# A recurrence followed by a token-and-channel mixer on one core: another order of the first batch's work, and another layout of the last branch

## The chip, the cores and the metric

The program runs on one core of a Trainium2 chip. The core has five engines with an instruction stream each: PE (TensorE, matrix products into PSUM banks), DVE (VectorE), ACT (ScalarE), POOL (GpSimd) and SP (SyncE, which here issues nearly all DMAs). [...] The metric is the device time of one launch in microseconds (us), the median of several runs; lower is better.

## The reference

```
for t in range(S):                                   # S = 768, batch 4, 8 heads of 48
    y[:, :, t] = r_t @ (state + (u * k_t) outer v_t)
    state = w_t[..., None] * state + k_t outer v_t
x = y, heads side by side                            # (4, 768, 384)
h = relu(x^T @ w_tok1) @ w_tok2                      # 768 -> 256 -> 768, over tokens
x = x + h^T
out = x + relu(x @ w_ch1) @ w_ch2                    # 384 -> 1536 -> 384, over channels
```

All is float32 for the kernel. The four weight matrices come as float64 and are turned to float32 on the chip.

## The kernel before

**Units.** The recurrence is cut into twelve units: a batch (4) times half of a sequence of 6 blocks of 128 tokens, so three units a batch (`UB = 3`, `NU = 12`; unit 0, 1, 2 are the first batch, written `e0`, `e1`, `e2`). A unit has four chunks of 64 tokens. `unit(i)` returns its steps as functions:

- `ends` (L351 to L357): a scan on DVE over the decays, and a reciprocal. `begins` (L364): a second scan. `keys` (L361) and `queries` (L367): products on DVE.
- `own_u` (L372, L264): four products by u on ACT. `own_gram`, `gram` (L248): 32 small products each on PE into a pair of banks of `ps_g`. `mask` (L406) and `own_put` (L260): DVE reads these into `at`.
- `tokens` (L278): eight turns of the keys on PE into two banks of `ps_m`; `copied` (L279): two copies to `kT` on ACT.
- `carry` (L295): the outer products `kv` of keys and values on PE. `scaled` (L419, four small ACT instructions) multiplies a state by the chunk's decay; `updates` (L429, DVE) adds the chunk's part of `kv` and makes the next state. So the chunks of a unit, and the units of a batch, form one chain: state, scaling, state.
- `before` (L308, PE: queries times states) and `after` (L322, PE: `at` times values) sum into one `y` in `ps_a`, a pool of one pair of banks, which most units' `kv` use too. Between the two stands the ACT copy `seen` (L314). `taken` (L328): three ACT copies of `y` into `x`.
- `ranges` (L348): two ACT instructions over 1041 columns, each of which sums up into `flags` whether a decay left the range in which this way of computing holds.

**Weights.** `convert` turns a block of float64 to float32: `load` (L197, two DMAs into `spare` or `scratch`), `exponent` (L200, DVE), `mantissa` (L206, DVE), `raise_two` (L203, ACT), `add` (L212, DVE), `signs` (L209, ACT) and `put` (L215 and two L218, DVE; L215 reads what L203 and L209 made). In the first batch's list these are `x`, `m`, `p`, `add`, `g`, `put` with the number of the block. Three blocks make the token weights, nine the channel weights (`to_ch`).

**Mixer.** `hidden` (L497, with L499 on ACT), `back` (L504 on PE, L506 on DVE adds to `x`), `turn` (L512, L513), `up` (L520 on PE, L522 on ACT) and `down` (L591), or `quarters` (L609), which makes a product with seven smaller ones, and the stores (L596, L613).

**Order.** `strict` gives PE, DVE and ACT exactly the order of the calls. For the three units of the first batch that order is one list written by hand (L700 to L709). SP's order is left to the scheduler of the language. After that list PSUM is dealt out anew (`ps_m` gets six banks), and for every batch `woven` merges lists of (cost, function) by the share of the cost sum that lies ahead of each: the next batch's unit steps among this batch's mixer pieces. `ahead` is the list of the first mixer's `turned` pieces, `both` that of its first 24 `up` pieces.

**End.** `verdict` sums `flags` on PE and DVE to one number. Every engine loads it (L768) and compares (L835). If a decay was out of range, everything is computed again in another way (`by_halves`, in a loop); with the inputs of the reference this doesn't happen. The layout is: compare, then an unconditional jump over the loop, which on each engine waits for that engine's own last work (on SP: for all DMA semaphores), then the loop's code, then the end (L868).

Of the kernel before, what the change touches and what calls it, by code (L numbers as in the profile page):

```python
# [10 lines left out]
f32 = mybir.dt.float32  # L11
bf16 = mybir.dt.bfloat16
i32 = mybir.dt.int32
# [15 lines left out]
ROWS = P + D  # L29
# [33 lines left out]
def rwkv6_then_mixer(  # L63
# [17 lines left out]
    nc = tc.nc  # L81
# [28 lines left out]
    def bank(name):  # L110
        return ps_m.tile([128, 512], f32, name=name, tag="m")
# [16 lines left out]
    def load_w(i):  # L128
        if i < NU:
            for cols in (slice(MID, WCOLS), slice(0, MID)) if i == 0 else (slice(0, WCOLS),):  # L130
                sp.dma_start(ws[i % 2][:, cols], w[i][:, cols])

    def load_rk(i):
        if i < NU:
            for n in (1, 0):
                for rows in (slice(0, 128),) if i < 3 else (slice(0, D), slice(P, P + D)):
                    sp.dma_start(rks[i % 3][rows, ts(n, COLS)], rk[i, n, rows, :])

    vs, nears = {}, {}

    def load_v(i):
        if i < NU:
            vs[i] = vpool.tile([128, UC, DM], f32, name="vt")
            b, j = divmod(i, UB)
            sp.dma_start(vs[i], v[b, ts(j, UC * 128), :].rearrange("(c p) e -> p c e", p=128))
# [138 lines left out]
            f()  # L284
        return kT

    def outer(kT, vt, half, where=None):

        where = where or (ps_a, "a")
        kv = where[0].tile([128, 2, 512], f32, name="kv_ps", tag=where[1])  # L290
        for c in range(UC):
            for a in range(A):
                for j, q in ((0, 0), (1, 1), (0, 1), (1, 0)):
                    if 2 * (half * UC + c) + j < 2 * C - 1:
                        pe.matmul(kv[ts(q, P), j, ds((c * A + a) * D, D)], kT[ts(j, T), c, a, ts(q, P)],  # L295
                                  vt[ts(j, T), c, ts(2 * a + q, D)], start=True, stop=True)
        return kv

# [31 lines left out]
    def unit(i):  # L330
# [75 lines left out]
                dve.tensor_mul(at[:, q], g, over_heads(strictly, g.shape[1]))  # L406

        def carry():
            L["kv"] = outer(L.pop("kT"), vs[i], half, (ps_g, "gram") if i == UB - 1 else (ps_a, "a"))

        def by_last(c, j):
            return of_chunks(L["to_end"], 1, 1)[:, :, 0].rearrange("p (x j) -> p x j", j=2)[:, ts(c, A), j]
# [8 lines left out]
        def update(c, j):  # L421
            g = 2 * (half * UC + c) + j
            if g < 2 * C - 1:
                new = state[bt, g + 1] = apool.tile([128, A, D], f32, name="state", bufs=3)
                got = L["kv"][:ROWS, j, ds(c * A * D, A * D)].rearrange("p (a e) -> p a e", a=A)
                if g == 0:
                    dve.tensor_copy(new[:ROWS], got)
                else:
                    dve.tensor_add(new[:ROWS], L["before"][g][:ROWS], got)  # L429
# [32 lines left out]
    def weight_sums(n):  # L462
        t1, t2, t4 = w_sums
        to, a, b = ((t1, w12, w11), (t2, w22, t1), (t4, w21, t2), (w12, w22, w12))[n]
        dve.tensor_sub(to, a, b)
# [203 lines left out]
    def steps(i):  # L669
# [29 lines left out]
    t0, t1, t2 = (e["scaled"] for e in (e0, e1, e2))  # L699
    strict(*e0["own_u"], e0["ends"], e0["own_gram"], e0["begins"], e0["keys"], e0["tokens"], *e0["copied"], e0["queries"], lambda: load_w(2),  # L700
           e0["gram"], *e1["own_u"], e1["ends"], e0["carry"], *e0["ranges"], e0["mask"], e0["own_put"], e1["own_gram"], s0[0], t0[1],
           x0, p0, s0[1], t0[2], m0, g0, e1["begins"], s0[2], t0[3], add0, s0[3], e0["before"], put0, load2,
           e1["keys"], e0["after"], *e0["taken"], e1["tokens"], *e1["copied"], e1["queries"], e1["gram"], *e2["own_u"], t1[0],
           e2["ends"], e1["carry"], lambda: load_v(2), e2["begins"], e1["mask"], e2["own_gram"], e1["own_put"], x1, p1, s1[0], t1[1],
           m1, g1, e2["keys"], s1[1], t1[2], e2["tokens"], e2["queries"], s1[2], t1[3], e2["gram"], *e2["copied"], h[0], h[1], add1, s1[3],
           t2[0], e1["before"], e2["mask"], e2["carry"], e1["after"], e2["own_put"], put1, s2[0], t2[1],
           *e1["taken"], h[2], h[3], x2, s2[1], t2[2], m2, p2, *h[4:6], add2, g2, s2[2], t2[3], *h[6:8], s2[3], e2["before"], put2, e2["after"],
           *e2["taken"], lambda: (load_w(3), load_rk(3), load_v(UB), load_w(4), load_rk(4)), to_ch[0][0], to_ch[1][0],
           *e1["ranges"], *h[8:], *e2["ranges"], lambda: sp.dma_start(u_rows, u_all))  # L709

    six_banks.close()
    ps_g, ps_m = None, six_banks.enter_context(tc.tile_pool(name="ps_m", bufs=6, space=bass.MemoryType.PSUM))
# [4 lines left out]
    flagged = []  # L717

    def verdict():
        total = bank("total")[0:1, :2 * NU]  # L720
        pe.matmul(total, ones, flags.rearrange("p i n -> p (i n)"), start=True, stop=True)
        of_all = const.tile([128, 1], f32, name="of_all")
        beyond = const.tile([128, 1], i32, name="beyond")
        dve.tensor_reduce(out=of_all[0:1], in_=total, axis=mybir.AxisListType.X, op=ALU.add)
        dve.tensor_scalar(beyond[0:1], of_all[0:1], 0.0, 1.0, op0=ALU.is_le, op1=ALU.is_lt)
        flagged.append(beyond)

    def last_mixing():
        hiddens, turned, rights, thirds, quarters = mixing_of(B - 1)
        of, sums = rights(0)  # L730
        *turned, end = turned
        pieces = [e for h in hiddens for e in h] + turned[:8] + sums[:4] + turned[8:10] + sums[4:8] + turned[10:] + sums[8:]
        ups = thirds(0, of)
        of, sums = rights(1)
        pieces += ups[:2] + [end] + ups[2:4] + woven(ups[4:], sums) + thirds(1, of)

        def third():
            L["of"], L["sums"] = rights(2)

        L = {}  # L740
        sums = [(0.05, lambda n=n: L["sums"][n][1]()) for n in range(12)]
        lefts_of = [(0.9, lambda n=n: L["ups"][n][1]()) for n in range(15)]
        pieces += [(0.01, third)] + woven(quarters(0), sums) + [(0.1, verdict), (0.01, lambda: L.update(ups=thirds(2, L["of"])))]
        return pieces + lefts_of + quarters(1) + quarters(2)

    for bt in range(B):
        ahead = []
        if bt == 0:
            to_ch = [single(e, n) for n, e in enumerate(to_ch)]
            both = [f for e in zip(ups[0], ups[1]) for f in e]  # L750
            ahead = woven(turned, sum(to_ch[:2], []))
            of_weights = [(0.1, lambda n=n: weight_sums(n)) for n in range(4)]
            pieces = woven(both, sum(to_ch[2:8], [])) + woven(downs[0][:6], to_ch[8]) + woven(downs[0][6:], of_weights[:3])
            pieces += downs[1][:4] + of_weights[3:] + downs[1][4:] + ups[2] + downs[2]
        elif bt < B - 1:
            hiddens, turned, ups, downs = mixing_of(bt)
            pieces = [e for h in hiddens for e in h] + turned
            *pieces, last = pieces
            ups[0].insert(2, last)
            for s in range(S // SEG):  # L760
                pieces += ups[s] + downs[s]
        else:
            pieces = last_mixing()
        n = (bt + 1) * UB
        att = [e for i in range(n, n + UB) if i < NU for e in steps(i)]
        strict(*(f for _, f in ahead + (woven(att, pieces) if att else pieces)))

    rare = nc.values_load(flagged[0][0:1, 0:1], min_val=0, max_val=1, skip_runtime_bounds_check_because="a comparison's result")  # L768

    def by_halves(b):  # L770

# [17 lines left out]
        for half in range(UB):  # L789
# [25 lines left out]
            for c in range(UC):  # L815
                for j in range(2):
                    g = 2 * (half * UC + c) + j
                    if g < 2 * C - 1:
                        new = states[g + 1] = apool.tile([128, A, D], f32, name="before", bufs=5)
                        got = kv[:ROWS, j, ds(c * A * D, A * D)].rearrange("p (a e) -> p a e", a=A)  # L820
                        if g == 0:
                            dve.tensor_copy(new[:ROWS], got)
                        else:
                            dve.tensor_mul(new[:ROWS], states[g][:ROWS], by[:, ts(c, A), j].unsqueeze(2).to_broadcast([ROWS, A, D]))
                            dve.tensor_add(new[:ROWS], new[:ROWS], got)
# [6 lines left out]
        for s in range(S // SEG):  # L832
            emit(ups[s] + downs[s])

    with tc.If(rare > 0, preferred_fallthrough_block=False):  # L835
        with tc.For_i(0, B, 1) as b:
            by_halves(b)

# [33 lines left out]
```

## Time and profile before

| what | value |
|---|---|
| median of 3 runs | 546.42 us (545.99 to 547.14) |
| the profiled execution | 544.09 us, of it 542.3 us span |
| busy in the span | PE 505.3, DVE 335.9, ACT 212.4, POOL 1.3 us |
| mean granted PE clock | 0.972 |
| DVE busy in 0:10, 10:20, 20:30, 30:40, 40:50, 50:60 | 6.93, 9.36, 9.90, 9.36, 9.09, 2.59 us |
| ACT busy in the same | 3.19, 7.93, 4.81, 6.67, 6.81, 8.20 us |
| PE busy in the same | 1.41, 6.93, 6.64, 6.11, 8.76, 7.59 us |
| granted PE clock in the same | 1.00, 0.85, 0.50, 0.67, 0.95, 1.00 |

The span reaches from the program's first instruction to its last; the launch around it makes the rest of the time. A share is an average over stages with different limits: the first 60 us hold the first batch's recurrence and the token weights, up to about 145 us the first mixer runs beside the channel weights' conversion and the second batch's units, and then three mixers follow, the first two of them with the next batch's units beside them. PE's busy time is modelled: 10.00 of 10 us doesn't mean that PE is at its peak.

### The profile page before, as it was taken

Reading aid. Unit: us, or ns where it says so; the run is one execution under the profiler, and the core shown is the slowest. Engines: PE = TensorE matmul, PEld = TensorE weight load, DVE = VectorE, ACT = ScalarE, POOL = GpSimd, SP = SyncE. Lnnn points to the kernel's source line nnn. Section 1 sums busy time; section 2 is a strip of 40 time slices with the busy share of each in tenths; the row PEclk is TensorE's granted clock in tenths of the full one; section 3 lists DMA queues with packets and bytes.
Section 4 is the critical chain, followed back from the end, with each engine's and each line's share of the span. In section 5 each row is a group of like instructions: output and inputs, shape, how many; then the busy total and the mean of one; then the engine's idle time right before and its main releaser. Section 6 shows DMA issues by size and latency. Waiting matters only on the chain.

```text
span 542.3 us, 12629 instructions
## 1 busy us (share of the span) xinstructions
PE 505.3 (93%) x5542; PEld 436.7 (81%) x5542; DVE 335.9 (62%) x514; ACT 212.4 (39%) x525; POOL 1.3 (0%) x10
## 2 busy tenths in 40 slices
PE   3578899899799999999899999999999999999995
PEld 3466478676798968898898967898898968999995
DVE  7998499878771754193381655286394625775653
ACT  3676876671233323424324333523414313531300
POOL 0000000000000000000000000000000000000000
PEclk9669999999999999999999999999999999999998
DMA  8968656623221404204123113002000000000000
GB/s 307 332 157 242 183 167 242 174 89 97 84 74 61 132 15 129 59 7 152 30 64 122 33 58 100 30 1 89 2 29 2 2 29 1 1 1 31 1 31 33
DMA packets 20941, 46.01 MB, mean 85 GB/s; under 512 B 2128, under 2 KB 13008, under 8 KB 20880
## 3 DMA queue, kind: packets, MB, share of 16 engines
q1 hardware_dynamic: 20736, 45.14, 26.1%
q8 instruction: 45, 0.74, 0.6%
q14 instruction: 16, 0.13, 0.1%
q10 hardware_dynamic: 144, 0.00, 0.0%
HBM read 40.41 MB, written 4.72 MB: 83 GB/s over the span
## 4 chain that ended last, share of the span: by engine, by line
PE 75%; DVE 15%; ACT 4%; DMA 3%; issue 2%; SPq 0%; DVEq 0%; ACTq 0%
PE q_ps L609 26%; PE z_ps L520 21%; PE z_ps L552 6%; PE h_ps L504 5%; PE h_ps L497 5%; PE y_ps L322 3%; PE y_ps L308 3%; DMA rk<-in_rk_dram 2%; PE gram L248 2%; DVE scratch L212 2%; PE kv_ps L295 1%; DVE wch L218 1%; PE k_ps L278 1%; DVE w L364 1%; PE xT_ps L512 1%
## 5 line engine op out<-in xcount | busy, mean ns | idle before, releaser
L520 PE MATMUL z_ps<-xT,wch 128*128 128x256 f32 x648 | 148.0, 384 | 0.0
L520 PEld LDWEIGHTS z_ps<-xT,wch 128*128 128x128 f32 x648 | 121.0, 190 | 16.6 <-DVE wch L218 0.3
L609 PE MATMUL q_ps<-wch,z 128*128 128x192 f32 x492 | 87.8, 330 | 0.0
L609 PEld LDWEIGHTS q_ps<-wch,z 128*128 128x128 f32 x492 | 81.1, 191 | 1.3 <-DVE z L651 0.3
L522 ACT ACTIVATE z<-z_ps 128x256 f32<-128x256 f32 x108 | 41.1, 381 | 84.0 <-PE z_ps L520 83.3
L419 ACT ACTIVATE before<-state,to_end 112x48 f32<-112x48 f32 x176 | 44.2, 324 | 32.6 <-DVE state L429 29.9
L609 PE MATMUL q_ps<-scratch,z 128*128 128x192 f32 x324 | 56.5, 327 | 0.2 <-DVE z L651 0.2
L609 PEld LDWEIGHTS q_ps<-scratch,z 128*128 128x128 f32 x324 | 53.0, 190 | 0.6 <-issue 0.4
L429 DVE TENSOR_TENSOR state<-before,kv_ps 112x192 f32<-112x192 f32 x40 | 14.0, 350 | 40.1 <-ACT before L419 28.1
L504 PE MATMUL h_ps<-h,wtok 128*128 128x384 f32 x96 | 35.4, 493 | 0.6 <-ACT h L499 0.6
L497 PE MATMUL h_ps<-x,wtok 128*128 128x384 f32 x96 | 32.5, 490 | 2.8 <-ACT x L328 2.6
L506 DVE TENSOR_TENSOR x<-x,h_ps 128x384 f32<-128x384 f32 x24 | 13.3, 553 | 34.1 <-PE h_ps L504 33.9
L619 DVE TENSOR_TENSOR o<-x,z 128x192 f32<-128x192 f32 x8 | 2.9, 359 | 49.2 <-ACT z L618 46.7
L497 PEld LDWEIGHTS h_ps<-x,wtok 128*128 128x128 f32 x96 | 17.8, 190 | 14.6 <-ACT x L328 3.4
L356 DVE TENSOR_TENSOR_SCAN to_end<-w,starts 112x1041 f32<-112x1041 f32 (+1 forms) x13 | 28.1, 2160 | 2.2 <-DMA w<-in_w_dram 1.8
L364 DVE TENSOR_TENSOR_SCAN w<-w,starts 112x1041 f32<-112x1041 f32 x12 | 27.9, 2321 | 0.1
L348 ACT ACTIVATE junk<-to_end,least 112x1041 uint8<-112x1041 f32 x12 | 14.0, 1163 | 28.3 <-DVE to_end L356 28.3
L504 PEld LDWEIGHTS h_ps<-h,wtok 128*128 128x128 f32 x96 | 16.6, 190 | 10.1 <-ACT h L499 2.8
L328 ACT COPY x<-y_ps 64x384 f32<-64x384 f32 (+1 forms) x36 | 17.1, 474 | 19.1 <-PE y_ps L322 18.8
L308 PEld LDWEIGHTS y_ps<-before,rk 48*64 48x64 f32 x704 | 13.5, 139 | 13.4 <-issue 8.0
L308 PE MATMUL y_ps<-before,rk 48*64 48x48 f32 x704 | 15.1, 227 | 9.6 <-DVE state L429 9.6
L513 ACT COPY xT<-xT_ps 128x384 f32<-128x384 f32 x24 | 11.4, 476 | 22.8 <-PE xT_ps L512 22.8
(136 smaller groups left out, 671.3 us busy)
## 6 DMA issues: line engine op xcount, KB each, us to landing
rk<-in_rk_dram SPq DMA_DIRECT2D x36, 192.0 KB, 4.1
near<-in_near_dram SPq DMA_DIRECT2D x8, 768.0 KB, 4.4
w<-in_w_dram SPq DMA_DIRECT2D x11, 520.5 KB, 3.4
spare<-in_w_ch_dram SPq DMA_DIRECT2D x10, 512.0 KB, 4.8
vt<-in_v_dram SPq DMA_DIRECT2D x12, 384.0 KB, 3.9
out_dram<-o SPq DMA_DIRECT2D x24, 192.0 KB, 1.9
scratch<-in_w_ch_dram SPq DMA_DIRECT2D x8, 512.0 KB, 4.6
rk<-in_rk_dram SPq DMA_DIRECT2D x6, 512.0 KB, 8.5
```

Of the source, the lines that this page charges most:

```text
L308: pe.matmul(y[put(q, j), q, ds((c * A + a) * D, D)], r_[q * P:q * P + D, ds((c * A + a) * 128 + j * T, T)], before[g][q * P:q * P + D, a, ...
L322: pe.matmul(y[put(q, j), q, ts(ca, D)], at[ts(j, T), q, ca, :], vt[ts(j, T), c, ts(2 * a + q, D)], start=False, stop=ca == 0, skip_group_c ...
L328: return [lambda: act.copy(x[:, 0], got[:, 0])] + [lambda n=n: act.copy(x[ts(n, P), 1], got[ts(1 - n, P), 1]) for n in range(2)]
L356: dve.tensor_tensor_scan(to, of, start, 0.0, op0=ALU.mult, op1=ALU.add)
L364: dve.tensor_tensor_scan(w_[:ROWS], w_[:ROWS], starts[:ROWS], 0.0, op0=ALU.mult, op1=ALU.add)
L419: act.mul(t[:ROWS, a], state[bt, g][:ROWS, a], by_last(c, j)[:, a:a + 1])
L497: pe.matmul(sums[i], wtok1[:, c, ts(i, 128)], x_of()[:, c, :], start=(c == 0), stop=(c == C - 1))
L504: pe.matmul(ps, wtok2[:, i, ts(c, 128)], h1[:, i, :], start=(i == 0), stop=(i == DTOK // 128 - 1))
L520: pe.matmul(ps, wch1[:, m, ts(jt, 128)], xT[:, m, ts(s, SEG)], start=(m == 0), stop=(m == DM // 128 - 1))
L522: act.activation(zs[s][:, jt, :], ps, AF.Relu)
L552: pe.matmul(ps[:, q], lefts[r][:, ts(q, 128)], of[r], start=first and q == 0, stop=end and q == JB - 1, skip_group_check=True)
L609: pe.matmul(ps, a[:, j, :], b[:, j, :], start=(j == 0), stop=(j == HJ - 1))
```

## The change

It has three parts.

1. **The first batch's list.** Unit 0's steps stay in place. Then the states of units 1 and 2 follow each other without conversions between unit 1's: `t1[0]` comes right after unit 0's last state, `e1["carry"]` goes ahead of unit 0's `taken`, unit 2's `own_u`, `ends`, `keys`, `tokens` and `carry` go ahead of unit 1's `before`; the second and third block of token weights move behind them. Unit 2's `kv` no longer takes a pair of banks of `ps_g` but two single banks of `ps_m`, so `outer` returns a list of two and its readers index it.
2. **Flag sums.** `ranges` of unit 1 leave the list for `ahead`, those of unit 2 for the first six pieces of `both`. The cost sums of both lists grow by that.
3. **The branch.** `verdict` yields 1 for within range, the compare jumps for that case to a block at the end of the code, and the loop is its other side. Four pieces ahead of the end of the last mixer's products PE gets a hint that names this jump as likely taken.

```diff
-    def outer(kT, vt, half, where=None):
-
-        where = where or (ps_a, "a")
-        kv = where[0].tile([128, 2, 512], f32, name="kv_ps", tag=where[1])
+    def outer(kT, vt, half, apart=False):
+
+        both = None if apart else ps_a.tile([128, 2, 512], f32, name="kv_ps", tag="a")
+        kv = [bank("kv_ps") if apart else both[:, j] for j in range(2)]
...
-           x0, p0, s0[1], t0[2], m0, g0, e1["begins"], s0[2], t0[3], add0, s0[3], e0["before"], put0, load2,
-           e1["keys"], e0["after"], *e0["taken"], e1["tokens"], *e1["copied"], e1["queries"], e1["gram"], *e2["own_u"], t1[0],
-           e2["ends"], e1["carry"], lambda: load_v(2), e2["begins"], e1["mask"], e2["own_gram"], e1["own_put"], x1, p1, s1[0], t1[1],
-           m1, g1, e2["keys"], s1[1], t1[2], e2["tokens"], e2["queries"], s1[2], t1[3], e2["gram"], *e2["copied"], h[0], h[1], add1, s1[3],
-           t2[0], e1["before"], e2["mask"], e2["carry"], e1["after"], e2["own_put"], put1, s2[0], t2[1],
-           *e1["taken"], h[2], h[3], x2, s2[1], t2[2], m2, p2, *h[4:6], add2, g2, s2[2], t2[3], *h[6:8], s2[3], e2["before"], put2, e2["after"],
-           *e2["taken"], lambda: (load_w(3), load_rk(3), load_v(UB), load_w(4), load_rk(4)), to_ch[0][0], to_ch[1][0],
-           *e1["ranges"], *h[8:], *e2["ranges"], lambda: sp.dma_start(u_rows, u_all))
+           x0, p0, s0[1], t0[2], m0, g0, e1["begins"], s0[2], t0[3], add0, s0[3], t1[0], e0["before"], put0, load2,
+           e1["keys"], e0["after"], *e2["own_u"], e1["tokens"], *e1["copied"], e1["queries"], e1["carry"], *e0["taken"], lambda: load_v(2),
+           e1["gram"], e2["ends"], e2["keys"], s1[0], t1[1], e2["tokens"], e2["begins"], e2["copied"][0], s1[1], t1[2], e2["copied"][1],
+           e2["carry"], e1["mask"], s1[2], t1[3], e1["own_put"], e2["own_gram"], s1[3], t2[0], e2["queries"], e2["gram"], e1["before"],
+           s2[0], t2[1], x1, p1, m1, e1["after"], s2[1], t2[2], e2["mask"], *h[:4], s2[2], t2[3], e2["own_put"], *e1["taken"], add1, g1,
+           s2[3], e2["before"], put1, to_ch[0][0], e2["after"], *h[4:8], x2, m2, *e2["taken"], p2, add2, g2, *h[8:], put2,
+           lambda: (load_w(3), load_rk(3), load_v(UB), load_w(4), load_rk(4)), to_ch[1][0], lambda: sp.dma_start(u_rows, u_all))
...
-        dve.tensor_scalar(beyond[0:1], of_all[0:1], 0.0, 1.0, op0=ALU.is_le, op1=ALU.is_lt)
+        dve.tensor_scalar(within_range[0:1], of_all[0:1], 0.0, None, op0=ALU.is_le)
...
+        ending = quarters(2)
+        ending.insert(-5, (0.01, lambda: tc.mark_branch_hint_location("by_halves", "LikelyTaken", [pe.engine])))
...
-            ahead = woven(turned, sum(to_ch[:2], []))
+            ahead = woven(turned, sum(to_ch[:2], []), [(1.3, f) for f in e1["ranges"]])
+            both = woven(both[:6], [(1.3, f) for f in e2["ranges"]]) + both[6:]
...
-    with tc.If(rare > 0, preferred_fallthrough_block=False):
+    with tc.If(common > 0, preferred_fallthrough_block=False, label="by_halves") as within_range:
+        pass
+    with within_range.Else():
         with tc.For_i(0, B, 1) as b:
             by_halves(b)
```

More of the change, by code (lines that the diff above doesn't have):

```diff
@@ L294, in outer @@
                     if 2 * (half * UC + c) + j < 2 * C - 1:
-                        pe.matmul(kv[ts(q, P), j, ds((c * A + a) * D, D)], kT[ts(j, T), c, a, ts(q, P)],
+                        pe.matmul(kv[j][ts(q, P), ds((c * A + a) * D, D)], kT[ts(j, T), c, a, ts(q, P)],
                                   vt[ts(j, T), c, ts(2 * a + q, D)], start=True, stop=True)
@@ L408, in carry @@
         def carry():
-            L["kv"] = outer(L.pop("kT"), vs[i], half, (ps_g, "gram") if i == UB - 1 else (ps_a, "a"))
+            L["kv"] = outer(L.pop("kT"), vs[i], half, apart=i == UB - 1)
         def by_last(c, j):
@@ L424, in update @@
                 new = state[bt, g + 1] = apool.tile([128, A, D], f32, name="state", bufs=3)
-                got = L["kv"][:ROWS, j, ds(c * A * D, A * D)].rearrange("p (a e) -> p a e", a=A)
+                got = L["kv"][j][:ROWS, ds(c * A * D, A * D)].rearrange("p (a e) -> p a e", a=A)
                 if g == 0:
@@ L722, in verdict @@
         of_all = const.tile([128, 1], f32, name="of_all")
-        beyond = const.tile([128, 1], i32, name="beyond")
+        within_range = const.tile([128, 1], i32, name="within_range")
         dve.tensor_reduce(out=of_all[0:1], in_=total, axis=mybir.AxisListType.X, op=ALU.add)
-        dve.tensor_scalar(beyond[0:1], of_all[0:1], 0.0, 1.0, op0=ALU.is_le, op1=ALU.is_lt)
-        flagged.append(beyond)
+        dve.tensor_scalar(within_range[0:1], of_all[0:1], 0.0, None, op0=ALU.is_le)
+        flagged.append(within_range)
     def last_mixing():
@@ L743, in last_mixing @@
         pieces += [(0.01, third)] + woven(quarters(0), sums) + [(0.1, verdict), (0.01, lambda: L.update(ups=thirds(2, L["of"])))]
-        return pieces + lefts_of + quarters(1) + quarters(2)
+        ending = quarters(2)
+        ending.insert(-5, (0.01, lambda: tc.mark_branch_hint_location("by_halves", "LikelyTaken", [pe.engine])))
+        return pieces + lefts_of + quarters(1) + ending
     for bt in range(B):
@@ L766, in rwkv6_then_mixer @@
         strict(*(f for _, f in ahead + (woven(att, pieces) if att else pieces)))
-    rare = nc.values_load(flagged[0][0:1, 0:1], min_val=0, max_val=1, skip_runtime_bounds_check_because="a comparison's result")
+    common = nc.values_load(flagged[0][0:1, 0:1], min_val=0, max_val=1, skip_runtime_bounds_check_because="a comparison's result")
     def by_halves(b):
@@ L819, in by_halves @@
                         new = states[g + 1] = apool.tile([128, A, D], f32, name="before", bufs=5)
-                        got = kv[:ROWS, j, ds(c * A * D, A * D)].rearrange("p (a e) -> p a e", a=A)
+                        got = kv[j][:ROWS, ds(c * A * D, A * D)].rearrange("p (a e) -> p a e", a=A)
                         if g == 0:
```

## The prediction

> **What bounds the kernel now.** I read the page first (engine shares, the slices, the chain), then the chain of waits in order of time for 50 to 150 us, then the timeline of 0 to 150 us, and last the branch's own line.
>
> The page: TensorE is busy in 93% of the span and the chain is 75% PE, but the slices show that this is not so at the start. The DVE row has its eights and nines there.
>
> ```profile
> span 542.3 us, 12629 instructions
> PE   3578899899799999999899999999999999999995
> DVE  7998499878771754193381655286394625775653
> PEclk9669999999999999999999999999999999999998
> PE 75%; DVE 15%; ACT 4%; DMA 3%; issue 2%; SPq 0%; DVEq 0%; ACTq 0%
> ```
>
> So a change of the first batch is worth what it moves on the DVE and ACT chains before about 150 us; after that PE runs back to back and all shifts with its start. The list of waits of 0 to 90 us holds one long hole of the DVE:
>
> ```profile
> DVE x L506 <- PE h_ps L504: 6.7, 1, 6.7
> ```
>
> It lies at 54.3 to 61.0: the conversions of token weights are finished, the DVE has nothing but the mixer's first addition, and that waits through this part of the chain (start, length, what):
>
> ```profile
> 53.18 1.19 PE y_ps L322 x64
> 54.40 0.48 ACT x L328
> 55.87 1.26 ACT junk L348 x2
> 57.16 1.26 ACT junk L348 x2
> 58.41 0.86 ACT h L499 x2
> 59.32 2.86 PE h_ps L504 x8
> 62.76 1.13 DVE scratch L212
> ```
>
> From 62.76 the chain is DVE with little between. Two places behind it matter here, from the timeline; both are unit outputs y for which PE stands idle until the DVE's last state is there:
>
> ```profile
> 104.10 1.14 PE L308 MATMUL y_ps<-before,rk 48*64 48x48 f32 x48 [2.60 <-DVE state L429]
> 145.22 1.15 PE L308 MATMUL y_ps<-before,rk 48*64 48x48 f32 x64 [2.39 <-DVE state L429]
> ```
>
> The end: the branch's line (count: shortest/median/longest ns, first to last start).
>
> ```profile
> L835 PEldq COMPARE_BRANCH  x2: 95/1724/3353, 534.2 to 536.9; - x2
> L835 SPq EVENT_SEMAPHORE  x8: 17/17/17, 538.1 to 540.4; - x8
> ```
>
> PE's jump at 536.86 takes 3.35 us. SP waits until 540.4 for the DMA semaphores; the last store was issued at 537.08. Its sixteenth landing is 3.15 us after issue, its fifteenth 1.85; the ten stores before it are complete in 1.84 to 1.97 each.
>
> [...] in its DMA records a 16,384-byte instruction packet runs 537.81 to 538.98, inside PE's 3.35 us. [...] eight packets of the last store start only at 538.975, when that instruction packet is through, while the other 120 are done by 538.6. [...] Here y's L322 takes 1.93 us after the 2.6 us hole at 104, against 1.08 in later batches.
>
> **The change, part by part.**
>
> *First batch.* Until unit 0's last state (22.80) the order is the same. I go forward with durations of the timeline, each engine in the order in which the changed program issues: a state L429 0.35, its scaling L419 x4 1.0, a scan 2.25, keys or queries 1.15, mask or pick 1.2, L203/L209 1.05 to 1.15, copies of y 1.45, of kT 0.5 each.
> - ACT: unit 2's u-products from 25.5 to 27.1, then kT's copies, which wait for PE's turns (end 29.36): 29.95; then y's copies to 31.4. These free the one bank pair that y and kv share, and kv of unit 1 starts at 31.4 (before 30.84). Behind that wait on PE stand unit 1's gram and unit 2's turns; nobody asks for them before 35. The DVE meanwhile does unit 2's scan and keys (31.1) and waits to 32.0.
> - Unit 1's states: 32.0, 34.7 (behind the scan), 36.8 (behind a kT copy), 38.3. Before, 35.36 to 40.94: 2.7 earlier.
> - The pick ends at 38.2 and frees a gram bank. PE then has two grams and y of unit 1; queries end at 39.7. Each takes 1.1 at full and 1.8 at half clock; with 1.45, y ends at 42.6 (before 43.9).
> - The copy `seen` stands on ACT ahead of unit 2's second scaling, which also needs y for its buffer. Behind it: 43.8, 45.8 (an exponent between), 47.2. Before, the last scaling ended at 52.5.
> - Unit 2's kv now lies in two banks of `ps_m`, the only two, so the first four hidden matmuls wait on PE for its third state (46.1), and unit 2's y behind them. They end at 47.8, before the copies that y needs: nothing, and up to 1.3 if those copies came first.
> - Unit 1's y copies 48.6, signs 49.7, unit 2's y 49.7, within 51.1 (54.3 before), copies 52.6. Only four matmuls of hidden are left, not eight: 53.9. ACT does exponent and signs first (54.8), h at 55.7 against 59.27.
> - The DVE now has two conversions here: sign at 49.7, L215 and two L218 to 51.6, the next whole one to 56.8, L200, and L506 at 57.4; at half clock 58.6. I take 57.8 against 60.99: **3.2 us earlier**. The wait of 6.7 becomes work; what is late next is the DVE itself. SP's first load of w_ch moves from 41.1 to about 49.7, behind loads of rk, w and v. It lands in 4.8 (median of its row), about 55.5 for both pieces, before L200 at 57, with 1.5 to spare. The second is issued at 54.8 and needed at 64. The loads of v for unit 2 and of `u_rows` move on SP too; their readers (kv of unit 2 at 37, products after 125) are far off.
>
> *Flag sums.* Four L348 of 1.28 each. In the hole they cost nothing: beside PE's hidden, or before the first L203. Now two stand on ACT between L203 and L209 of the first two w_ch conversions. From L200's end: ACT 1.12+1.28+0.42+1.13=3.95; DVE until L215 3.2 in the first, 2.7 in the second. So L215 waits 0.8 and 1.3: **2.1 us back**. The other two stand beside a scan of 2.25, or before an L203 whose L200 is not done: nothing, at most 2.6.
>
> So w_ch's third block, for which PE's z L520 waits, comes 1.1 earlier than 71.3.
>
> *The weave.* Unit steps and mixer pieces of the first batch are merged by their cost sums; these changed, so unit 3's y stands one z earlier (after 19 of 24), unit 4's one product earlier. At both PE waits for the DVE, and one z (1.3 us) or one product (0.98) more comes after the wait: the hole grows at the front. At 104: the DVE 1.1 earlier, and some 0.9 of its waits for L209 (0.66 and 0.94 at 90.8 and 96.8) go, as signs now stand one z earlier on ACT; less 1.3: **0.7 earlier**. At 145: 0.3 gained (a state ahead of the wait for an output store), 0.98 later, of which 0.8 fills PE's wait for `seen`: about 0.6. From there PE is back to back: **-0.6** at the end of this part. Bounds: -3.2 (nothing of it given back) to +2.9.
>
> *The end.* PE's jump is now taken at the compare (534.2), before the drain[...]. Either is enough to have the fetch over before the last store's packets (538.4). The store then lands in 1.85, not 3.15: **-1.3**. SP's further chain, 540.25 to 542.3, stays. PE's arrival at 540.27 would have been the next limit and goes with it. The compare with one condition less, and the hint, are single small instructions ahead of filled queues: nothing. On DVE, ACT, POOL and SP the jump comes before their last waits instead of after; they took 0.04 to 0.06 us. Bounds: 0[...] to -1.4.
>
> Sum on the profiled execution: span 542.3, and 544.09 with what lies around it; -0.6-1.3=-1.9 gives 542.2. The runs' median is 546.42, 2.3 above that execution; the difference is carried over: **544.5**.
>
> **Rivals.**
> - *All is kept*: ACT's slack swallows the sums and the weave's loss is met by PE's clock. For it: the DVE is the longer engine until 104. Against: L215 already meets L209 within 0.05 us at 69.95. 546.42-3.2-1.3=541.9.
> - *Only the end*: what the first batch wins is eaten by sums and weave. 545.1. Or the end fails too, and -0.6 alone stays: 545.8.
> - *Slower: the sums become the bound.* All four L348 fall on the DVE's chain, 5.1, and the first batch brings its half-clock value less ACT's queue, 2.2: 546.42+2.9-1.3=548.0. It decides once more than 4.6 us of sums and weave come back. For it: ACT then has L203, L209, z and sums between 72 and 79 without a gap. Against: z has six banks, and PE needs a z evicted only every 1.3.
>
> **How the numbers follow.** Forecast 0.42 (own range 543.3 to 545.4), all kept 0.22, only the end or only the start 0.22, slower 0.14. Range 541.6 to 546.6 leaves out the slower case. A run here tells 0.2% (1.1 us) from no change: faster takes the forecast, all kept and some of the third: 0.68; same 0.18; slower 0.14.
>
> **What would show it.** Right: the wait of 6.7 gone and L506 first at 57.4 to 58.6; L215 waiting about 0.8 and 1.3 for L209; y of unit 3 near 102 with PE idle about 3 before it; a PE branch under 0.2 us and SP's last wait ending near 1.9 after the last issue. Wrong: L506 after 59.5, PE idle before z for more than before, or the last store again at 3 us.

## The result, and the profile after

| | before | after |
|---|---|---|
| median of 12 runs each | 546.88 us | 545.92 us |
| lowest to highest | 545.14 to 548.77 | 542.25 to 547.62 |
| after by before | | 0.9976, 95% interval 0.9955 to 0.9996 |
| profiled execution: its time, its span | 544.09, 542.3 us | 542.25, 540.5 us |
| mean granted clock of TensorE in it | 0.972 | 0.981 |

Faster by 0.24%: 1.3 us by the ratio, 1.0 by the medians. The forecast was 544.5, 1.9 below its base. One thing has to be known before the trace is read: the profiled execution is the fastest of the changed kernel's twelve, and its clock of 0.981 is well above their median of 0.968. What it shows at the start is a good case. Two runs of one experiment (sums in holes) were in a slower state, with a lower granted clock (0.961 and 0.952), and are left out of its median.

The page after (span, busy tenths of PE, DVE and the granted clock in 40 slices, shares of the chain):

```profile
span 540.5 us, 12631 instructions
PE   3468889899799999999899999999999999999997
DVE  7987899878671755194372656277295525775654
PEclk9689999899899999999999999999999999999999
PE 83%; DVE 11%; ACT 4%; issue 1%; DMA 1%; DVEq 0%; ACTq 0%
```

PE's share of the chain went from 75% to 83%, DVE's from 15% to 11%. Much of that lies between 77 and 92 us and between 113 and 126 us, where the chain was mostly the DVE's and is now PE's; around 51 us it ran through PE and ACT already before. The list of waits of 0 to 90 us has for the two waits that the prediction speaks of:

```profile
DVE x L506 <- PE h_ps L504: 0.8, 1, 0.8
DVE scratch L215 <- ACT scratch L209: 3.6, 4, 1.3
```

The hole of 6.7 is gone, as forecast. But L506 doesn't follow the DVE's own work, it still waits 0.8 for PE. The chain of waits there (start, length, what):

```profile
51.00 5.37 PE h_ps L497 x16
56.40 0.50 ACT h L499
56.94 2.86 PE h_ps L504 x8
59.82 0.56 DVE x L506
...
66.08 1.24 ACT junk L348 x2
67.69 1.04 ACT scratch L209
68.75 0.70 DVE scratch L215
```

L506 first starts at 58.60 (60.99 before). And at 66.08 one of the moved flag sums is on the chain, ahead of L209 and L215. The row of L215 above holds four waits, two of them in the token weights; those of the first two conversions of w_ch, which the prediction speaks of, are seen in the DVE's timeline, of the kernel before and then of the changed one:

```profile
64.30 0.69 DVE L215 TENSOR_TENSOR scratch<-scratch 128x1024 bf16<-128x1024 bf16 x1
69.99 0.69 DVE L215 TENSOR_TENSOR scratch<-scratch 128x1024 bf16<-128x1024 bf16 x1
```

```profile
61.91 0.68 DVE L215 TENSOR_TENSOR scratch<-scratch 128x1024 bf16<-128x1024 bf16 x1
68.75 0.69 DVE L215 TENSOR_TENSOR scratch<-scratch 128x1024 bf16<-128x1024 bf16 x1 [1.09 <-ACT scratch L209]
```

PE's timeline a little later, of the kernel before and then of the changed one, shows what that does, and a second hole that wasn't foreseen:

```profile
70.55 9.38 PE L520 MATMUL z_ps<-xT,wch 128*128 128x256 f32 x42
79.77 1.04 PE L278 MATMUL k_ps<-ident,rk 128*128 128x128 f32 x8
```

```profile
70.23 5.88 PE L520 MATMUL z_ps<-xT,wch 128*128 128x256 f32 x26 [1.04 <-DVE wch L218]
77.06 1.09 PE L278 MATMUL k_ps<-ident,rk 128*128 128x128 f32 x8 [0.95 <-DVE rk L361]
```

Before, PE did z without a pause and then turned unit 3's keys. Now it stops 1.04 us for the third block of weights, and 0.95 us for the keys of unit 3, whose turns stand two z earlier in its order (after 5 of the 24 instead of 7). Where y of units 3 and 4 follow:

```profile
102.51 1.14 PE L308 MATMUL y_ps<-before,rk 48*64 48x48 f32 x48 [2.01 <-DVE state L429]
...
143.44 1.15 PE L308 MATMUL y_ps<-before,rk 48*64 48x48 f32 x64 [3.54 <-DVE state L429]
144.51 3.80 PE L609 MATMUL q_ps<-scratch,z 128*128 128x192 f32 x12
148.25 1.19 PE L322 MATMUL y_ps<-vt,at 64*64 64x48 f32 x64
```

At 143.44 the changed kernel is 1.78 us ahead (145.22 before), but its hole is 3.54 (2.39), and the product that was done ahead of the hole before now runs behind it in 3.80 (the granted clock was 0.50 from 144.97 to 148.38). The first output of the products made with seven smaller ones (the first L647) comes at 153.57, against 153.54. From there to the last L647 (536.72 and 536.70) the two traces are at most 0.03 apart. So in this pair nothing of the first batch's lead is left, and all the gain is at the end:

```profile
L837 PEldq COMPARE_BRANCH  x1: 397/397/397, 534.3 to 534.3; - x1
L837 SPq EVENT_SEMAPHORE  x8: 17/17/17, 538.6 to 539.2; - x8
```

PE's jump is taken at 534.3 in 0.40 us. The last store's sixteenth landing is 1.86 us after its issue (3.15 before), and SP jumps at 538.1, ahead of its waits, so that the 0.49 us between its jump and its next instruction lie under the store. From the last L647 to the end of the span: 5.61 before, 3.82 after. The DMA records fit: the kernel before has 16,384-byte instruction packets at 537.81 to 538.98, inside PE's jump and beside the last store, and at 541.23 to 542.18; the changed kernel has them at 526.84 to 528.06 and at 535.38 to 536.38, both before its last store is issued at 537.10. Which engine a packet is for, the records don't say.

### The profile page after: what moved, and what is told of

It is laid out like the page before. It is cut to its first block, busy times and chain, and to the rows that moved or that the text cites. A ratio compares the mean times of both kernels' runs of the same rounds, so it can differ in the third digit from the quotient of the medians.

```text
span 540.5 us, 12631 instructions
## 1 busy us (share of the span) xinstructions
PE 503.2 (93%) x5542; PEld 434.2 (80%) x5542; DVE 335.9 (62%) x514; ACT 212.4 (39%) x525; POOL 1.3 (0%) x10
## 4 chain that ended last, share of the span: by engine, by line
PE 83%; DVE 11%; ACT 4%; issue 1%; DMA 1%; DVEq 0%; ACTq 0%
PE q_ps L609 27%; PE z_ps L520 24%; PE z_ps L552 6%; PE h_ps L497 5%; PE h_ps L504 5%; PE gram L248 3%; PE h_ps L591 3%; PE y_ps L308 3%; PE y_ps L322 2%; PE kv_ps L295 2%; PE k_ps L278 2%; DVE to_end L356 1%; PE xT_ps L512 1%; DVE w L364 1%; ACT before L419 1%
## 5 line engine op out<-in xcount | busy, mean ns | idle before, releaser
L609 PE MATMUL q_ps<-scratch,z 128*128 128x192 f32 x324 | 58.1, 333 | 0.0
L609 PEld LDWEIGHTS q_ps<-scratch,z 128*128 128x128 f32 x324 | 54.4, 194 | 0.2
L506 DVE TENSOR_TENSOR x<-x,h_ps 128x384 f32<-128x384 f32 x24 | 13.3, 552 | 28.2 <-PE h_ps L504 28.1
```

What stands on the lines that cost most here:

```text
L609: pe.matmul(ps, a[:, j, :], b[:, j, :], start=(j == 0), stop=(j == HJ - 1))
```

## The experiments

Each ran beside the kernel before on the same chip; its median in the three groups of runs was 545.75 (53 runs), 546.58 (44) and 546.42 (35), and 545.94 (17) for the last one. The second and the third group ran on one chip, the others on two more.

### The end alone, the turn alone, the rest alone

Branch only: the kernel before with part 3 of the change.

```diff
-    with tc.If(rare > 0, preferred_fallthrough_block=False):
+    with tc.If(common > 0, preferred_fallthrough_block=False, label="by_halves") as within_range:
+        pass
+    with within_range.Else():
...
+        ending.insert(-5, (0.01, lambda: tc.mark_branch_hint_location("by_halves", "LikelyTaken", [pe.engine])))
```

> The kernel before with the third part of the change alone (branch turned, hint). Theory (the end alone carries the gain, the first batch's gain is given back by the weave): the last addition L647 stays at 536.7 us, the jump on PE is under 0.5 us, the last store's sixteenth landing comes at 1.9 us, and the span is 540.5: 1.8 less than before, ratio about 0.9967, the same as the whole change. Rival (the first batch brings 0.6 on most runs): about 1.3 to 1.8 less, but clearly behind the whole change.

Median 543.66 (16 runs), ratio 0.9958 (0.9935 to 0.9981). Last L647 to the end 3.82, last landing 1.86 after issue, and PE's jump is short:

```profile
L837 PEldq COMPARE_BRANCH  x1: 402/402/402, 536.8 to 536.8; - x1
```

Turn only: the same without the hint.

```diff
-        ending.insert(-5, (0.01, lambda: tc.mark_branch_hint_location("by_halves", "LikelyTaken", [pe.engine])))
```

> The kernel before with the branch turned around but without the hint to PE. Theory (turning is enough, since the jump and its fetch then stand ahead of PE's drain): PE's jump takes about 3.35 us from 534.2, so PE is at the end by 537.7, and its 16 KB fetch is through by 536.4, before the last store's packets: span 540.5. Rival (the hint is what saves): the fetch still meets the last store, landing at about 3 us, span 541.8 to 542.3.

One run of 543.66. The line of its branch:

```profile
L835 PEldq COMPARE_BRANCH  x1: 3345/3345/3345, 535.5 to 535.5; - x1
```

The jump still takes 3.35 us without the hint, as it did before, but it is issued 2.9 us ahead of the last store (538.40), a 16,384-byte instruction packet runs inside it at 536.52 to 537.45, and the store lands in 1.98. Last L647 to the end is 3.94. So in these single profiles turning the branch does 1.67 of the 1.79, the hint the last 0.1.

List only: the changed kernel with the old branch (parts 1 and 2).

```diff
-    with tc.If(common > 0, preferred_fallthrough_block=False, label="by_halves") as within_range:
-        pass
-    with within_range.Else():
+    with tc.If(rare > 0, preferred_fallthrough_block=False):
...
-        ending.insert(-5, (0.01, lambda: tc.mark_branch_hint_location("by_halves", "LikelyTaken", [pe.engine])))
```

> The changed kernel with the branch as it was before: first batch, flag sums and their weave alone. Theory: first addition L506 at 58.6 instead of 61.0, output of unit 4 begun 1.8 earlier, and nothing left of it from 154 us on: last addition at 536.7, span 542.3, ratio 1.000. Rival: 0.6 us or more left at the end, ratio 0.999 or below.

Median 547.31 (22 runs), ratio 1.0018 (1.0001 to 1.0036). Its profile has L506 at 63.35 and a jump of 4.13 us, last landing 3.85. The two ratios multiply to 0.9976, which is what the whole change gives. So the end brings 0.42%, 2.3 us, and the first two parts cost 0.18%, 1.0 us (0.1 to 2.0 by the interval), where the prediction had them at -0.6.

### What comes back: sums and weave

Old weave: the changed kernel, with unit 2's sums counted at nothing in the merge, so that unit steps and mixer pieces meet as before.

```diff
             both = woven(both[:6], [(1.3, f) for f in e2["ranges"]]) + both[6:]
+            both = [(0.0 if f in e2["ranges"] else c, f) for c, f in both]
```

> The changed kernel, but the two flag sums in the first six up pieces count nothing in the cost sum, so unit steps and mixer pieces meet in the same order as before the change; all else as changed. Theory (the weave gives the gain back: a product of 1.95 us stands behind PE's wait at unit 4's output instead of ahead of it): that product is ahead again, PE waits 1.6 to 2.4 us less work behind it, and everything from 154 us on lies about 1.6 earlier: last addition at 535.1, span 538.9, ratio about 0.994. Rival (PE's half clock after the wait gives it back, whatever the weave): last addition at 536.7, span 540.5, as in the changed kernel.

Median 545.03 (22 runs), ratio 0.9977 (0.9958 to 0.9996): no different from the change itself; the 0.994 of its theory did not come. The median doesn't show what the weave costs; but L506 came at 62.46 here, and the stretch behind it was shorter, which led to the measure below.

Sums in holes: the changed kernel with the four flag sums back in the list, in three holes of ACT; PE and DVE keep their order.

```diff
-  ... e1["carry"], *e0["taken"], ...
+  ... e1["carry"], *e0["taken"], e1["ranges"][0], ...
-  ... s1[3], t2[0], e2["queries"], ...
+  ... s1[3], t2[0], e1["ranges"][1], e2["ranges"][0], e2["queries"], ...
-  ... to_ch[0][0], e2["after"], ...
+  ... to_ch[0][0], e2["ranges"][1], e2["after"], ...
-            ahead = woven(turned, sum(to_ch[:2], []), [(1.3, f) for f in e1["ranges"]])
+            ahead = woven(turned, sum(to_ch[:2], []), [(1.3, lambda: None) for n in range(2)])
-            both = woven(both[:6], [(1.3, f) for f in e2["ranges"]]) + both[6:]
+            both = woven(both[:6], [(1.3, lambda: None) for n in range(2)]) + both[6:]
```

> The changed kernel, its four flag sums L348 moved back into the list, into ACT's holes (behind unit 0's copies, two ahead of the `seen` of unit 1, one behind that of unit 2); their shares of 1.3 in both merges stay as empty pieces, so PE and DVE keep the changed order. Theory A (the sums cost at L215): L215 waits at most 0.1 for L209 in the first two conversions of w_ch, where the changed kernel waited 0 and 1.09; from L506 to the third block of z some 1.1 less (11.6 before, 10.5 here); median about 0.5 to 1.1 under the changed kernel's in the same runs. Theory B (the sums cost nothing that lasts): the wait goes, but y of unit 4 waits for its last state as long or longer, first L647 within 0.3 of where L506 puts it in the changed kernel, median within 0.5.

Median 542.47 (12 runs), ratio 0.9931 (0.9907 to 0.9954). PE's timeline:

```profile
69.50 6.81 PE L520 MATMUL z_ps<-xT,wch 128*128 128x256 f32 x30
77.26 1.09 PE L278 MATMUL k_ps<-ident,rk 128*128 128x128 f32 x8 [0.95 <-DVE rk L361]
```

The hole at the third block is gone, so the sum ahead of L209 made it; the hole ahead of L278 stays, so the weave made that one. y of unit 4 still has its 3.54. The median is 2.8 below that of the changed kernel on this chip (545.31), more than the 1.1 that the stretch below shows; its median clock was 0.976 against 0.972 too, and why is not settled.

Sums in holes, old weave: the same without the empty pieces in the two merges.

```diff
-            ahead = woven(turned, sum(to_ch[:2], []), [(1.3, lambda: None) for n in range(2)])
+            ahead = woven(turned, sum(to_ch[:2], []))
-            both = woven(both[:6], [(1.3, lambda: None) for n in range(2)]) + both[6:]
```

> As the run before, and without the empty pieces: unit steps and mixer pieces of the first batch meet as in the kernel before, y of unit 3 behind one z more, y of unit 4 behind one product more. Theory A (sums and weave both cost): fastest of the four, 1 to 2 under the changed kernel, PE idle ahead of y of unit 4 under 2.5 (3.54 in the changed kernel) and of unit 3 about 2.6. Theory B (the clock sets it; holes only move): within 0.7 of the changed kernel's median.

Median 540.83 (7 runs), ratio 0.9913 (0.9873 to 0.9952).

```profile
68.32 9.38 PE L520 MATMUL z_ps<-xT,wch 128*128 128x256 f32 x42
77.54 1.04 PE L278 MATMUL k_ps<-ident,rk 128*128 128x128 f32 x8
...
141.38 1.93 PE L308 MATMUL y_ps<-before,rk 48*64 48x48 f32 x64 [2.38 <-DVE state L429]
```

Both holes are gone, and the third is back at 2.38. Once more:

> The version with the flag sums in ACT's holes and the old weave once more, for its interval and a second profile. If sums (1.1) and weave (1.5) are the whole loss: L506 to the fourth L647 218.4 to 218.7 again (221.1 to 221.2 in the changed kernel), ratio to the kernel before 0.990 to 0.994, whatever the half-clock windows do to L506 itself (58.6 to 63.4).

Median 541.33 (9 runs), ratio 0.9917 (0.9881 to 0.9953). This version is 4 to 6 us below the kernel before, and below the changed kernel: 540.83 and 541.33 against 545.92 and 545.31. The interval of the changed kernel's first comparison (0.9955 to 0.9996) lies above both of its intervals; that of the second, below, overlaps them by under 0.001. The difference on this chip, 4.0 to 4.5 by the medians, is again more than the stretch below accounts for (2.5). Against branch only (0.9960 on this chip, below) the ratios are 0.0043 and 0.0047 lower: without the sums' and the weave's cost the list is worth some 2.3 to 2.6 us, though these intervals overlap.

Weave alone: branch only, and two empty pieces of 1.3 in the merge, so that PE's order from the mixer on is the changed one.

```diff
+            both = woven(both[:6], [(1.3, lambda: None) for n in range(2)]) + both[6:]
             pieces = woven(both, sum(to_ch[2:8], []))
```

> The kernel before with the branch turned and hinted, and with two empty pieces of 1.3 in the merge of the first batch: PE's order from the mixer on is that of the changed kernel, while the list and the place of the flag sums are those of before. If the weave alone costs 1.5: L506 to the fourth L647 at 219.8 to 220.3 (218.5 in the kernel before and with the branch alone), PE idle about 3.5 ahead of y of unit 4 (2.39 before), one product L609 between it and L322, and the median 0.8 to 2 above that of the branch alone (543.66, twice). If the weave costs only together with the changed list: 218.4 to 218.7, and the median within 0.7 of the branch alone.

Median 545.53 (13 runs), ratio 0.9975 (0.9947 to 1.0003): above the branch alone by 1.9 by the medians, which come from different chips, and by 0.8 to 0.9 by the ratios, whose intervals overlap. So here too the cost is read from the trace. L506 to the fourth L647 took 222.47, more than expected; but TensorE was at half clock for 13.65 us of that, against 6.83 in most others. Two of the holes, ahead of L278 and of y of unit 4, are as expected:

```profile
79.56 1.09 PE L278 MATMUL k_ps<-ident,rk 128*128 128x128 f32 x8 [0.96 <-DVE rk L361]
...
145.88 1.96 PE L308 MATMUL y_ps<-before,rk 48*64 48x48 f32 x64 [3.54 <-DVE state L429]
```

For a comparison of all traces, the stretch from L506 to the fourth L647 (about 60 to 280 us) is taken less half of PE's busy time in the half-clock windows of it, an estimate of its length at full clock, from the product that takes 3.80 us at half clock (the changed kernel's at 144.5) and 1.95 at full:

| kernel | the stretch | at full clock | PE idle in it |
|---|---|---|---|
| before; branch only, twice; turn only | 218.7; 220.2, 218.5; 218.6 | 215.1 to 215.3 | 8.1 to 8.3 |
| the change, twice; list only; keys turned twice (below) | 221.1, 221.2; 221.2; 222.8 | 217.7 to 217.8 | 10.2 |
| old weave | 219.7 | 216.3 | 9.2 |
| sums in holes | 220.1 | 216.7 | 9.2 |
| sums in holes, old weave, twice | 218.4, 218.7 | 215.2, 215.4 | 8.2, 8.3 |
| weave alone | 222.5 | 216.4 | 9.2 |

The change takes 2.5 us longer here than the kernel before. The sums are 1.0 to 1.1 of it (217.7 less 216.7 one way, 216.3 less 215.2 the other), the weave 1.2 to 1.5 (216.4 less 215.2; 217.8 less 216.3). With both undone it is as long as before. So whatever the list wins up to L506 has to be over 2.5 to be worth anything.

### Where L506 comes: the windows of the clock

The changed kernel and branch only, each once more on one chip:

> The changed kernel once more, for its profile and for a comparison on one chip with the others. If its L506 at 58.6 was the list's own: again 58.0 to 59.2. If it was a lucky phase of the half-clock windows: 60 to 63.5, with 20 us or more at half clock between 17 and 55 (13.7 in the first profile), and the later L506 in the profile with more half clock. Median near 545.5 against 546.5 of the kernel before; span less last addition 3.8.

> The kernel before with only the branch turned and its target hinted, once more, beside the changed kernel on one chip. If the list and the weave give nothing: median within 0.5 of the changed kernel's, both some 1.8 under the kernel before. If the list gives its 0.6 of the forecast: 0.6 above the changed kernel. If list and weave cost: at least 0.7 below it. Span less last addition 3.8 in each case.

Medians 545.31 (14 runs) and 543.66 (22), ratios 0.9969 (0.9946 to 0.9991) and 0.9960 (0.9940 to 0.9980). The intervals overlap, so this comparison alone wouldn't say that the first two parts cost something. L506 of the changed kernel came at 63.33 this time, not at 58.60, with the same instructions in the same order on every engine. Its windows (start:end, length, then busy time of PE, of its weight loads, DVE, ACT and POOL, the granted clock, DMA share, GB/s):

```profile
34.92:38.33 3.41, 1.88 (x42) 1.45 (x39) 3.41 (x5) 2.53 (x9) 0.00 (x0) 1.00 0.70 173
38.33:41.74 3.41, 3.22 (x107) 3.03 (x98) 1.20 (x3) 1.66 (x7) 0.00 (x0) 0.50 0.16 33
41.74:45.15 3.41, 2.29 (x86) 2.29 (x88) 2.54 (x4) 0.00 (x0) 0.00 (x0) 0.50 0.38 126
```

PE is busy for 1.88 of 3.41 in the first of these, 55%, and gets half a clock in the next. There and in the one after it is busy for 94 and 67%, and it stays at half clock until 51.98. In the first profile the windows lie otherwise (28.91, 32.33, 35.74 and so on), the three from 35.74 on are filled to 60 to 70%, and the clock stays full. Over the profiles of the changed list the place of L506 follows the time at half clock between 17 us and L506:

| | half clock | L506 |
|---|---|---|
| the change; sums in holes with old weave | 13.65 | 58.60; 58.76 |
| sums in holes; sums in holes with old weave again | 17.07 | 59.94; 59.99 |
| old weave | 27.31 | 62.46 |
| the change again; list only | 30.72 | 63.33; 63.35 |
| the old list, five profiles | 20.48 or 23.89 | 60.99 to 62.62 |

That is 0.28 us of L506 for each us at half clock (4.73 by 17.07). At the old list's 20.48 this line gives 60.5, 0.5 to 1.9 earlier than the old list.

The place of the windows says more still. Profiles of the changed list whose first stretch at half clock begins at the same time to 0.1 us agree in L506 to 0.2, wherever the flag sums stand: beginnings at 18.58 and 18.68 go with 58.76 and 58.60, at 20.17 and 20.25 with 59.99 and 59.94, at 17.80 and 17.85 with 63.35 and 63.33. The old list has 62.42 and 62.62 for beginnings at 18.49 and 18.51, but 62.14 at 17.80. So at one place of the windows the new list brings L506 some 3.8 us earlier, and at another 1.2 later. What it gains there on average, these profiles are too few to say.

To test the part of the windows, the changed kernel was given more work in these windows: unit 2's key transposes issued twice into the same banks.

```diff
-    def turned_keys(k_):
+    def turned_keys(k_, times=1):
...
-            for a in range(A):
+            for a in list(range(A)) * times:
...
-            L["kT"], L["copies"] = turned_keys(k_)
+            L["kT"], L["copies"] = turned_keys(k_, 2 if i == UB - 1 else 1)
```

> The changed kernel, with unit 2's eight key transposes L278 issued twice in a row into the same banks (0.5 us more PE work per kT copy at full clock, 1 at half). Theory C (the place of L506 is set by the half-clock windows: a full window that PE fills to about 0.55 or less is followed by a half one, one of 0.6 or more is not; a half window has to be filled to about 0.95): the repeats lift the windows around 32 to 39 over the edge, the stretch at half clock up to 52 doesn't occur, L506 comes at 58.5 to 60.5 (58.60 and 63.33 in the two profiles of the changed kernel), and the median falls by 0.5 to 2.5 under the changed kernel's 545.3 to 545.9. Theory D (no such edge; the extra matmuls only delay kT's copies): L506 spreads as before plus 0.5, between 59 and 64, median 0.3 to 1 above the changed kernel's.

Median 544.29 (22 runs), ratio 0.9953 (0.9933 to 0.9973); L506 at 60.74 with 17.07 us at half clock. The median fell by 1.0 and 1.6 against the two of the changed kernel, though it does more work, and the median clock rose to 0.977 (0.968 and 0.972). The intervals overlap, so the gain is not shown; and L506 lies a little outside the 58.5 to 60.5 expected. Its stretch at half clock begins at 20.10; at that place the versions with sums in holes and without the repeats had 59.94 and 59.99, 0.8 earlier. The same in the version with sums in holes and the old weave:

> Flag sums in ACT's holes, the old weave, and unit 2's key transposes twice. Theory C: L506 at 58.5 to 60.5, the median at or up to 0.5 under the same kernel without the repeats, with a narrower spread; L506 to the fourth L647 again 218.4 to 218.7. Theory D: median 0.3 to 1 above it.

Median 541.49 (12 runs), ratio 0.9905 (0.9874 to 0.9937), not below the 541.33 without it on the same chip; L506 at 59.73. Its windows lie within 0.17 us of those above; the one that answers to the first, and its next has a clock of 1.00 too:

```profile
34.76:38.17 3.41, 2.43 (x35) 2.07 (x30) 3.22 (x5) 2.18 (x8) 0.00 (x0) 1.00 0.67 161
```

The window at 34.8 is now filled to 71%, and the next keeps its full clock, as the theory of an edge has it: L506 comes at 59.73, against 63.33 and 63.35 at this place of the windows without the repeats. This fits repeats that help at one place of the windows and cost at another; but the flag sums stand elsewhere too in both comparisons, so it isn't shown. That it shortens the mean run is not shown in this version, whose median clock was 0.976 without the repeats and 0.977 with them. (Its stretch behind L506 took 220.8, not the 218.4 to 218.7 expected, with 13.65 us at half clock; at full clock it is 214.1, about 1 less than in the two profiles without the repeats, with 7.55 us of PE idle. Two half-clock windows lie around y of unit 4 there. What makes the difference stays open.)

## Why the prediction was right, and where not

The sign and the range held; the composition didn't. What was measured lies nearer to the rival "only the end" (545.1) than to the forecast, and the experiments show that it is this rival that happened: the total came out right by luck.

- **The end, -1.3.** Right in mechanism, 0.5 too small. "SP's further chain, 540.25 to 542.3, stays" failed: SP's jump with 0.49 us behind it moved ahead of its waits. The trace gives -1.79, the ratios of branch only 2.2 to 2.3. Of the 1.79, 0.50 is that and 1.29 the store. "Either is enough" holds of the turn for all but 0.1: alone it gives 1.67; the hint was not tried alone. PE's jump took 3353 ns before, 3345 turned without the hint, and 397 with it, not under 200 as forecast. SP's wait for the last store ends 1.9 after its issue, as forecast.
- **The first batch, -3.2.** The steps held up to 51 us: kv of unit 1 at 31.14 (31.4), its states at 32.36, 34.87, 36.56 and 38.03 (32.0, 34.7, 36.8, 38.3), y of unit 2 ending at 49.6 (49.7), copies from 51.07 to 52.5 (52.6). The term that failed is "Only four matmuls of hidden are left, not eight: 53.9", which is 2.5 us short. A matmul of this shape is two MATMUL records in the trace: eight of hidden's twelve stand behind unit 2's y, and the chain above has their sixteen records in 5.37. So hidden ends at 56.4, h at 56.9, and L506 waits for PE, not for the DVE: 58.60, which is the half-clock value only by chance, as the clock was full from 35.74 us on. And L506 spread not over 57.4 to 58.6 but over 58.6 to 63.35, with 13.65 to 30.72 us at half clock, in three of four profiles past the sign of being wrong, "L506 after 59.5". In the first pair of profiles the list gave 2.4 of the 3.2.
- **Flag sums, 2.1 back.** The mechanism was right, the size half of it: L215 waited 0 and 1.09 (0.8 and 1.3 forecast), and the traces price the sums at 1.0 to 1.1. That z's third block started at 70.23, as forecast (1.1 earlier than 71.3, 70.2), is luck: L506 was 0.8 later than assumed and the sums cost 1.0 less.
- **The weave.** The step that fell short is "one z (1.3 us) or one product (0.98) more comes after the wait", of which most was to be met again. With the list's smaller lead this step turned the sign of the first part. A product is twelve MATMUL records, 1.95 us at full clock and 3.80 at half, which is what it had at 144.5; and the turns of unit 3's keys, which stand not one but two z earlier, met a DVE that wasn't ready (0.95). Neither was in the sum. The cost is 1.2 to 1.5. y of unit 3 came at 102.51 with PE idle 2.01 (102 and 3 forecast). "PE idle before z for more than before" was named as a sign of being wrong, and it is there: 1.04 and 0.95, none before.
- **The sum.** -0.6 and -1.3 were forecast; -1.8 to -2.3 at the end and +1.0 (ratio 1.0018) ahead of it were found. Two errors of opposite sign kept the total within 1.4 us.

## What to carry to other kernels

A piece that is moved in a woven order costs where its neighbours then stand, not where it runs: put small side work into the holes of an engine's list, at no cost in the merge (here worth 2.5 us in the traces, and more by the medians), and see what moved past each wait. Before a gain is priced from one pair of profiles, read the clock windows of both; in these traces a stretch that leaves TensorE some 55 to 60% busy stands on an edge, and its time is a lottery (the changed list had L506 at 58.60 and at 63.33). And at the end of a program, try the jump ahead of the last wait: here the 16,384-byte instruction packets were then through before the last store, which landed in 1.86 to 1.98 us and not in 3.15.

## What wasn't expected of the hardware

The clock changes in windows of 3.41 us whose place differs from run to run: in fourteen profiles every stretch of one clock is a multiple of 3.41 us long (but for the last, which the record cuts off), and the borders lie at 28.91, 32.33 and 35.74 in one profile of the changed kernel and at 31.51, 34.92 and 38.33 in the other. How full the windows were is seen in these profiles between the first record of the clock (at 11.85 to 15.17 us) and 62 us. A full-clock window with PE busy for at most 53% was followed by a half one each time, one of 60% or more never; at 54 to 59% both occurred (57% ahead of a half one in the kernel before, 59.5% ahead of a full one in the changed). A half-clock window with at most 93% was followed by another one each time; of those with 94% or more 24 led to full clock and five (94 to 99%) did not. The longest idle gap in the window of 55% above is 1.24 us, and a half one followed. Busy times are modelled, so these are edges of this trace and not of the circuit.

By an estimate from the product that took 3.80 us at half clock and 1.95 at full, an extra half-clock window costs 1.7 us where PE is full, half of its length, and most of these profiles have one near 105 or one near 270 besides that near 147. That alone is 0.3% of the run, more than the change brings.
